# An mLSTM cell followed by a Fourier mix and an MLP: in batch 1, the order of the recurrence's products around the MLP's 64-feature products

## The chip, the cores and the metric

The kernel runs on one core of one Trainium2 chip. The metric is the device time of one execution in microseconds; the time before is the median of 11 runs. The profile is one further execution, in which the hardware profiler recorded every instruction.

The names used below are those of the profile: PE is TensorE (matmuls; PEld its weight loads), DVE is VectorE, ACT is ScalarE, POOL is GpSimd, SP is SyncE, whose queue issues all DMAs here. L465 is line 465 of the kernel before.

## What is computed

The reference has two parts. The first is a recurrence over 768 tokens for 4 batches of 8 heads with 40 features; the second, per batch, a Fourier transform over tokens and features, a normalization and an MLP with a residual.

```python
for t in range(S):                                  # mLSTM cell
    m_new = np.maximum(f_gate[:, :, t] + m, i_gate[:, :, t])
    f_stab, i_stab = np.exp(f_gate[:, :, t] + m - m_new), np.exp(i_gate[:, :, t] - m_new)
    C = f_stab * C + i_stab * np.einsum('bhd,bhe->bhde', vt, kt)
    n = f_stab * n + i_stab * kt
    h_tilde, nq = np.einsum('bhde,bhe->bhd', C, qt), np.einsum('bhd,bhd->bh', n, qt)
    y[:, :, t] = sigmoid(o_gate[:, :, t]) * h_tilde / np.maximum(np.abs(nq), 1.0)
...
u = x + np.real(np.fft.fft(np.fft.fft(x, axis=1), axis=2))   # x: y as (4, 768, 320)
un = (u - mean(u)) / np.sqrt(var(u) + 1e-06)
out = u + np.maximum(un @ w_ch1, 0.0) @ w_ch2                 # 320 -> 1280 -> 320
```

## The kernel before

**Chunks.** The recurrence isn't run token by token. A batch's 768 tokens are 6 chunks of 128, and each chunk needs, for its 8 heads: the *scores* of its keys with its queries (`mlstm_scores`, L465: 8 products with 40 rows, heads in pairs at partitions 0 and 64); a matrix of decays W (loaded by DMA, exponential on ACT in L421, cut to the causal half on POOL in L443 by `mlstm_mask`); the scores weighed by W (`mlstm_weigh`, DVE, L471); the queries times their decay, qg (`mlstm_scale_q`, POOL, L431); the *product with the state* (`mlstm_from_state`, L479: 4 full 128x128 products of C with qg); the *chunk outputs* (`mlstm_from_chunk`, L486: 8 products of the weighed scores with the values, 41 columns wide, into the same accumulator ph); and the *state update* (`mlstm_to_state`, L496: 8 products, 40 columns, into pc). The next state is made of the old one times its decay (`mlstm_decay`, POOL, L455) plus pc (`mlstm_gather`, DVE, L515; in chunk 0 a copy, L513). The same `mlstm_gather` copies ph to h on ACT (L517 to L529). `mlstm_turn` (L535) transposes h into px on PE, `mlstm_finish` (DVE, L544 to L550) divides and gates.

**The MLP's first layer.** In batch 0 it is done by `mlp_in`: 10 blocks of 128 hidden features for each of two groups of 3 chunks. The 320 inputs are 128 + 128 + 64, so a pair of blocks takes 4 full products (L837; 3 in the even slot, 1 in the odd one) and 2 products of 64 rows (L841, at partitions 0 and 64), called the 64-feature products. `mlp_relu` (ACT, L850) empties each pair.

**Order.** The kernel writes the order of all engines itself. `at(slot, phase, fn, ...)` puts a call into a table, and `run` goes through the table by slot and, in a slot, by phase; calls with the same key keep the order in which they were entered. The phases are EVAC = 0, FILL = 1, MAIN = 2, FILL_PE = 3, with fractions. Each engine executes its own instructions in the order so written. `plan_mlstm` enters a batch's recurrence; batch 1 begins at slot 32 with one chunk for every three slots, so that the scores of chunk c come in slot 32 + 3c, and the state product, the chunk outputs and the state update of chunk c three slots later, together with the next chunk's scores. Batch 0's `mlp_in` takes slots 31 to 50 in phase MAIN; the 64-feature products are in the even slots. Around them stand batch 0's last steps of the Fourier mix (L729 pu, L749 to L757 on DVE, L765 uc and L777 uT on ACT, the transpositions L772), the normalization factor (`mix_rstd`: L785 to L790 on DVE, then 12 small operations on POOL, L792 to L795, entered in slot 41), and the conversion of the second weight matrix from 64-bit floats (raw pieces by DMA; L344 and L346 on DVE, L351 and L352 on ACT, L358 to L364 on DVE).

**Buffers.** Two PSUM buffers (`ps_h`) are shared by ph, pc and px of all chunks, two (`ps_s`) hold scores, and four banks (`ps_m`) the rest; an instruction that writes a buffer waits for the last readers of what was in it.

Of the kernel before, what the change touches and what calls it, by code (L numbers as in the profile page):

```python
# [20 lines left out]
NT = S // L  # L21
# [29 lines left out]
def kernel(  # L51
# [70 lines left out]
    def at(slot, phase, fn, *args):  # L122
        plan.setdefault((slot, phase), []).append((fn, args))
# [7 lines left out]
    EVAC, FILL, MAIN, FILL_PE = range(4)  # L131
# [405 lines left out]
    def mlstm_finish(b, c):  # L537

        k = chunks.pop((b, c))
        if c == 0:  # L540
# [9 lines left out]
        nc.vector.tensor_tensor(out=xs[b][:, c, 0:DM].rearrange("p (h d) -> p h d", d=D), in0=h1[:, :, 0:D], in1=sc,  # L550
                                op=OP.mult)

    def plan_mlstm(b, s0, stride=3):
        for c in range(NT):
            s = s0 + stride * c
            if b > 0:
                t = 22 + 2 * c if b == 1 and c < 3 else s - 5
                at(t, FILL, mlstm_load, b, c)
                at(t, FILL, mlstm_load_max, b, c)
                at(t, FILL, mlstm_load_decay, b, c)  # L560
                at(s, FILL, mlstm_load_o, b, c)
            if (b, c) > (0, 0):
                at(s, FILL, mlstm_exp, b, c, 0)
                at(s + 1, FILL - 0.5, mlstm_exp, b, c, NP)
                last = (b, c) == (0, NT - 1)
                at(s - 1 if last else s, FILL_PE + (2.05 if last else 2), mlstm_scores, b, c)
                if b > 0:
                    at(s + 1, FILL, mlstm_mask, b, c)
            at(s, FILL, mlstm_scale_v, b, c)
            at(s if (b, c) == (0, 2) else s + 1, FILL + 0.1, mlstm_scale_q, b, c)  # L570
            at(s + 2, FILL, mlstm_decay, b, c)
            end = (b, c) == (0, NT - 1)
            at(s + 1 if end else s + 2, FILL - 0.4 if end else FILL, mlstm_weigh, b, c)
            at(s + 2 if end else s + 3, FILL_PE, mlstm_from_state, b, c)
            at(s + 2 if end else s + 3, FILL_PE + (2 if end else 3), mlstm_from_chunk, b, c)
            at(s + 3, FILL_PE + 3, mlstm_to_state, b, c)
            at(s + 3 if end else s + 4, FILL, mlstm_gather, b, c)
            if b == 0:
                t, x = ((8, 11), (11, 14), (13, 14), (14, 15.5), (17, 18), (18, 21))[c]
            else:  # L580
                t = s + (8, 8, 7, 5, 5, 5)[c]
                x = t + 1
            at(t, FILL_PE + ((2.5 if c < 4 else 1) if b == 0 else 1), mlstm_turn, b, c, b == 0 and c < 4)
            at(x, FILL + 0.05, mlstm_finish, b, c)


# [483 lines left out]
    def plan_batch(b, s_mlstm, s_mix, s_mlp):  # L1070
        plan_mlstm(b, s_mlstm)
        done = [s_mlstm + 3 * (j + NT // 2) + 7 for j in range(NT // 2)]
        assert s_mix >= done[-1] and s_mlp >= s_mix + 9
        late = [s_mlp + 2 * c for c in range(TG)]
        if b == 0:
            feat = [s_mix + 1, s_mix + 1, s_mlp + 3]
            turn = [s_mix + 2, s_mix + 3, s_mix + 4]
            add = turn + [s_mlp, s_mlp + 4, s_mlp + 6]
            late = [s_mlp + 2, s_mlp + 5, s_mlp + 7]
        else:  # L1080
            feat = [s_mix + c for c in ((3, 4, 6) if b == 1 else (3, 4, 7))]
            add = [s_mix + c for c in ((4, 4, 5, 6, 7, 7) if b == 1 else (4, 4, 5, 6, 8, 9))]
            turn = [s_mix + c for c in ((5, 6, 6) if b == 1 else (6, 7, 8))]
            late = [s_mix + c for c in ((7, 8, 8) if b == 1 else (9, 10, 10))]
            at(s_mlp, EVAC + 0.5, mlp_sums)
        plan_mix(b, s_mix, done, feat, add, turn + late)
        at(s_mlp + NFF, FILL + 0.6, mix_rstd, b)
        plan_mlp(b, s_mlp)
# [143 lines left out]
```

## Time and profile before

| What | us |
|---|---|
| Median of 11 runs | 421.61 |
| Lowest, highest | 421.40, 426.45 |
| Profiled execution, its own time | 421.59 |
| Span of the profiled execution | 419.9 |
| First to last full product of batch 0's first layer (L837) | 58.5 to 118.8 |

The span is the time between the first and the last recorded instruction; 1.69 us of the execution's time lie outside it.

In the stretch of the trace in which batch 0's first layer runs, the busy times were:

| Stretch, us | PE | PEld | DVE | ACT | POOL |
|---|---|---|---|---|---|
| 0 to 105 | 99.11 | 69.26 | 81.70 | 71.36 | 47.74 |
| 105 to 125 (20 us) | 19.36 | 12.62 | 18.99 | 11.18 | 8.38 |
| 125 to 150 (25 us) | 25.00 | 18.64 | 13.76 | 6.53 | 7.49 |

A timeline line gives start, duration, engine, line, operation, output and inputs, shape, and how many instructions were merged; what stands in brackets is the idle time of the engine before it and who ended it. Each fp32 matmul is recorded as two, so that "L837 x6" is three products. The durations of PE are modelled at their end; the distance from one start to the next is what was measured.

### The profile page before, as it was taken

How to read it: one execution, taken by the hardware profiler on the slowest of the kernel's cores; microseconds unless marked ns; L12 is line 12 of the kernel's file. 1: busy time of each engine (PE TensorE's matmuls, PEld its weight loads, DVE VectorE, ACT ScalarE, POOL GpSimd, SP SyncE). 2: the span in 40 equal slices, each digit the busy share in tenths (PEclk: the TensorE clock that was granted, in tenths of full speed). 3: DMA queues.
4: the chain of work that ended last, by engine and by line, in shares of the span. 5: the costliest groups of instructions: out<-in, count | busy, mean ns of one | idle time of the engine just before them, and what ended most of it. 6: DMA issues, size and time to landing. Idle time of an engine off the chain costs nothing.

```text
span 419.9 us, 8001 instructions
## 1 busy us (share of the span) xinstructions
PE 408.9 (97%) x2966; PEld 302.9 (72%) x2966; DVE 288.8 (69%) x682; ACT 189.5 (45%) x493; POOL 113.5 (27%) x194
## 2 busy tenths in 40 slices
PE   8999999999999999999999999999999999999997
PEld 6877555576667678776559998976559988455996
DVE  7789894767994738777765579788663786335652
ACT  6986276676562221664455413744441113355000
POOL 5654301459430620442131440341220000020000
PEclk9999999999999999999999999999999999999999
DMA  7789298557665254265100454210000000000010
GB/s 228 254 260 333 66 283 264 168 170 224 224 191 164 70 155 128 74 207 184 66 0 2 147 153 135 95 46 2 0 2 0 33 31 34 0 2 0 16 48 31
DMA packets 20549, 47.14 MB, mean 112 GB/s; under 512 B 2784, under 2 KB 9312, under 8 KB 20384
## 3 DMA queue, kind: packets, MB, share of 16 engines
q1 hardware_dynamic: 20512, 46.65, 35.6%
q8 instruction: 23, 0.38, 0.4%
q14 instruction: 14, 0.11, 0.1%
HBM read 42.52 MB, written 4.11 MB: 111 GB/s over the span
## 4 chain that ended last, share of the span: by engine, by line
PE 80%; DVE 9%; issue 3%; DMA 3%; ACT 2%; POOL 2%; ACTq 0%; DVEq 0%; POOLq 0%
PE pm L897 17%; PE po L999 17%; PE po L943 8%; PE pm L902 5%; PE ps L465 5%; PE ph L486 4%; PE ph L479 3%; PE pu L729 3%; PE pm L837 3%; PE px L535 2%; PE pz L698 2%; DMA kvt<-in_kv 1%; PE put L772 1%; PE pM L218 1%; PE pz L686 1%
## 5 line engine op out<-in xcount | busy, mean ns | idle before, releaser
L949 DVE SCALAR_TENSOR_TENSOR x<-po,rstd,x 128x160 f32<-128x160 f32 (+1 forms) x69 | 27.0, 394 | 40.5 <-PE po L999 34.1
L906 DVE TENSOR_TENSOR h<-h,pm 128x384 f32<-128x384 f32 x60 | 30.5, 550 | 30.5 <-ACT h L919 20.9
L421 ACT ACTIVATE W<-W,colT 128x128 f32<-128x128 f32 x144 | 45.0, 395 | 0.0
L443 POOL TENSOR_SCALAR_AFFINE_SELECT W<-W 128x1024 f32<-128x1024 f32 x18 | 21.5, 1197 | 79.8 <-ACT W L421 59.3
L943 PE MATMUL po<-w_sb,h 128*128 128x320 f32 x120 | 34.4, 435 | 0.0
L471 DVE TENSOR_TENSOR W<-ps,W 128x512 f32<-128x512 f32 x48 | 30.6, 679 | 4.2 <-POOL W L443 4.0
L897 PE MATMUL pm<-uT,w_sb 128*128 128x384 f32 x90 | 32.8, 492 | 0.2 <-DVE uT L885 0.2
L837 PE MATMUL pm<-uT,w_sb 128*128 128x384 f32 x80 | 29.8, 500 | 0.7 <-DVE x L749 0.5
L777 ACT COPY uT<-put 128x384 f32<-128x384 f32 x24 | 11.2, 478 | 40.2 <-PE put L772 40.2
L943 PEld LDWEIGHTS po<-w_sb,h 128*128 128x128 f32 x120 | 22.2, 190 | 9.5 <-issue 0.8
L999 PE MATMUL po<-T,S 128*128 128x160 f32 x180 | 27.9, 302 | 0.6 <-DVE x L949 0.6
L465 PE MATMUL ps<-qk 40*128 40x128 f32 x384 | 27.8, 284 | 0.0
L792 POOL TENSOR_TENSOR t<-rstd 128x6 f32<-128x6 f32 x12 | 3.0, 246 | 89.2 <-DVE v L790 88.6
L999 PEld LDWEIGHTS po<-T,S 128*128 128x128 f32 x180 | 25.5, 190 | 2.2 <-DVE x L949 1.0
L999 PE MATMUL po<-w_sb,h 128*128 128x160 f32 x180 | 26.4, 301 | 0.0
L465 PEld LDWEIGHTS ps<-qk 40*128 40x128 f32 x384 | 23.4, 187 | 4.2 <-issue 0.7
L999 PEld LDWEIGHTS po<-w_sb,h 128*128 128x128 f32 x180 | 25.1, 190 | 1.3 <-DVE x L949 0.3
L486 PE MATMUL ph<-W,kvt 128*41 128x128 f32 x384 | 25.8, 277 | 0.0
L524 ACT COPY h<-ph 41x512 f32<-41x512 f32 (+1 forms) x16 | 9.3, 583 | 35.7 <-PE ph L486 35.6
L431 POOL TENSOR_TENSOR qg<-qk,Gb 128x512 f32<-128x512 f32 x18 | 25.0, 1390 | 0.1
L479 PEld LDWEIGHTS ph<-qg,C 128*128 128x128 f32 x160 | 20.0, 191 | 6.3 <-issue 2.0
L897 PEld LDWEIGHTS pm<-uT,w_sb 128*128 128x128 f32 x90 | 16.2, 190 | 10.9 <-DVE h L906 1.5
(207 smaller groups left out, 866.8 us busy)
## 6 DMA issues: line engine op xcount, KB each, us to landing
W<-M_d SPq DMA_DIRECT2D x18, 512.0 KB
kvt<-in_kv SPq DMA_DIRECT2D x24, 324.0 KB
qk<-in_qkT SPq DMA_DIRECT2D x48, 160.0 KB
raw<-in_w SPq DMA_DIRECT2D x10, 640.0 KB
Gb<-G_d SPq DMA_DIRECT2D x36, 128.0 KB
so<-in_o SPq DMA_DIRECT2D x24, 160.0 KB
out<-x SPq DMA_DIRECT2D x24, 160.0 KB
ds_sb<-in_dft_s SPq DMA_DIRECT2D x1, 1155.0 KB
```

The costliest lines, as they stand in the source:

```text
L421: nc.scalar.activation(out=k.W[:, h, :], in_=M, func=AF.Exp, scale=-1.0, bias=colT[:, c, 0, b * H + h:b * H + h + 1])
L431: nc.gpsimd.tensor_tensor(out=k.qg, in0=k.qk[:, 0], in1=k.Gb, op=OP.mult)
L465: nc.tensor.matmul(k.ps[hip][:, p, :], k.qk[r, 1, p, :], k.qk[r, 0, p, :], start=True, stop=True)
L471: nc.vector.tensor_tensor(out=Wv, in0=k.ps[hip], in1=Wv, op=OP.mult)
L479: nc.tensor.matmul(k.ph[:, p, :], k.C[:, p, :], k.qg[:, p, :], start=(p == 0), stop=False, skip_group_check=True)
L486: nc.tensor.matmul(k.ph[hip * 64:hip * 64 + D1, p, :], k.v1[:, 2 * p + hip, :], k.W[:, 2 * p + hip, :], start=(c == 0 and p == 0), stop=Tr ...
L837: nc.tensor.matmul(k.pm[i], w1_sb[:, ch, f0:f0 + L], u[2 * ch], start=(ch == 0), stop=False)
L897: nc.tensor.matmul(bank, w, u, start=start, stop=True, skip_group_check=True)
L906: nc.vector.tensor_tensor(out=h, in0=h, in1=bank, op=OP.add)
L943: nc.tensor.matmul(k.po, hidden(gr, f)[:, i * L:(i + 1) * L], w2_sb[:, f, :], start=(f == 0), stop=(f == NFF - 1))
L949: nc.vector.scalar_tensor_tensor(out=u, in0=po, scalar=k.rstd[:, c:c + 1], in1=u, op0=OP.mult, op1=OP.add)
L999: nc.tensor.matmul(po, a[:, f], w[:, f], start=start and f == 0, stop=f == half - 1, skip_group_check=True)
```

## The change

In batch 1 alone (`b > 0`; the two lists of slots meet only batch 1's):

- `group(s)` moves slots 35 and 41 to 36 and 42. There the scores of chunks 1 and 3, and the chunk outputs and state updates of chunks 0 and 2 (with the gather behind them), run one slot later, behind the 64-feature products of that slot.
- In an even slot of batch 0's first layer, `mlstm_from_state` is entered at MAIN - 0.1, ahead of that slot's last full product, where it stood behind the 64-feature products (chunk 2's stood in slot 41, ahead of the scores of chunk 3, and is now in slot 42). This meets slots 36, 38, 42, 44 and 50 (in slot 36 chunk 0 has no product with the state). Slot 47 is odd and stays as it was.
- In a shifted slot's chunk the decay of the state on POOL is entered just behind the gather, and the gather at FILL + 0.05, behind the next chunk's weighing on DVE, behind the pair of `mlp_relu` or `mix` copies on ACT, and behind the next mask and qg on POOL.
- In an even slot `mlstm_turn` is entered at FILL_PE + 3.5 instead of FILL_PE + 1.

```diff
@@ -550,6 +550,14 @@
         nc.vector.tensor_tensor(out=xs[b][:, c, 0:DM].rearrange("p (h d) -> p h d", d=D), in0=h1[:, :, 0:D], in1=sc,
                                 op=OP.mult)
 
+
+
+    slots_of_halves = [s for s in range(32, 51, 2)]
+    shifted = (35, 41)
+
+    def group(s):
+        return s + (s in shifted)
+
     def plan_mlstm(b, s0, stride=3):
         for c in range(NT):
             s = s0 + stride * c
@@ -563,24 +571,26 @@
                 at(s, FILL, mlstm_exp, b, c, 0)
                 at(s + 1, FILL - 0.5, mlstm_exp, b, c, NP)
                 last = (b, c) == (0, NT - 1)
-                at(s - 1 if last else s, FILL_PE + (2.05 if last else 2), mlstm_scores, b, c)
+                at(s - 1 if last else group(s) if b > 0 else s, FILL_PE + (2.05 if last else 2), mlstm_scores, b, c)
                 if b > 0:
                     at(s + 1, FILL, mlstm_mask, b, c)
             at(s, FILL, mlstm_scale_v, b, c)
             at(s if (b, c) == (0, 2) else s + 1, FILL + 0.1, mlstm_scale_q, b, c)
-            at(s + 2, FILL, mlstm_decay, b, c)
+            at(s + 2, FILL + (0.1 if b > 0 and s in shifted else 0), mlstm_decay, b, c)
             end = (b, c) == (0, NT - 1)
+            g = group(s + 3) if b > 0 else s + 3
             at(s + 1 if end else s + 2, FILL - 0.4 if end else FILL, mlstm_weigh, b, c)
-            at(s + 2 if end else s + 3, FILL_PE, mlstm_from_state, b, c)
-            at(s + 2 if end else s + 3, FILL_PE + (2 if end else 3), mlstm_from_chunk, b, c)
-            at(s + 3, FILL_PE + 3, mlstm_to_state, b, c)
-            at(s + 3 if end else s + 4, FILL, mlstm_gather, b, c)
+            at(s + 2 if end else g, MAIN - 0.1 if b > 0 and g in slots_of_halves else FILL_PE, mlstm_from_state, b, c)
+            at(s + 2 if end else g, FILL_PE + (2 if end else 3), mlstm_from_chunk, b, c)
+            at(g, FILL_PE + 3, mlstm_to_state, b, c)
+            at(s + 3 if end else g + 1, FILL + (0.05 if g > s + 3 else 0), mlstm_gather, b, c)
             if b == 0:
                 t, x = ((8, 11), (11, 14), (13, 14), (14, 15.5), (17, 18), (18, 21))[c]
             else:
-                t = s + (8, 8, 7, 5, 5, 5)[c]
+                t = s + (8, 8, 7, 5, 5, 5)[c] + (c == NT - 1 and g > s + 3)
                 x = t + 1
-            at(t, FILL_PE + ((2.5 if c < 4 else 1) if b == 0 else 1), mlstm_turn, b, c, b == 0 and c < 4)
+            at(t, FILL_PE + ((2.5 if c < 4 else 1) if b == 0 else 3.5 if t in slots_of_halves else 1), mlstm_turn, b, c,
+               b == 0 and c < 4)
             at(x, FILL + 0.05, mlstm_finish, b, c)
 
 
```

## The prediction

> **What bounds the kernel now.** I read the page's busy times first, then the shares of the chain of waits, then the waits of PE, then the timelines of PE, DVE and POOL between 58 and 124 us, the stretch in which batch 0's first MLP layer and batch 1's recurrence run together. All of the change lies there: in the two built programs nothing before 69 us or after the last scores of this stretch changes its order.
>
> ```profile
> PE 408.9 (97%) x2966; PEld 302.9 (72%) x2966; DVE 288.8 (69%) x682; ACT 189.5 (45%) x493; POOL 113.5 (27%) x194
> PE 80%; DVE 9%; issue 3%; DMA 3%; ACT 2%; POOL 2%; ACTq 0%; DVEq 0%; POOLq 0%
> ```
>
> PE sets the time: what is taken off PE counts if PE doesn't wait instead. How a block's length depends on its neighbours is in PE's timeline:
>
> ```profile
> 61.27 0.92 PE L841 MATMUL pm<-uT,w1t_sb 64*128 64x384 f32 x4
> 62.02 1.06 PE L465 MATMUL ps<-qk 40*128 40x128 f32 x16
> 63.01 2.20 PE L837 MATMUL pm<-uT,w_sb 128*128 128x384 f32 x6
> ...
> 88.77 2.10 PE L837 MATMUL pm<-uT,w_sb 128*128 128x384 f32 x6
> 90.70 1.05 PE L479 MATMUL ph<-qg,C 128*128 128x128 f32 x8
> 91.69 1.16 PE L465 MATMUL ps<-qk 40*128 40x128 f32 x16
> 92.78 1.07 PE L486 MATMUL ph<-W,kvt 128*41 128x128 f32 x16
> 93.68 0.47 PE L496 MATMUL pc<-vw,kvt 128*40 128x41 f32 x16
> 94.09 0.91 PE L837 MATMUL pm<-uT,w_sb 128*128 128x384 f32 x2
> 94.93 0.92 PE L841 MATMUL pm<-uT,w1t_sb 64*128 64x384 f32 x4
> 95.78 2.20 PE L837 MATMUL pm<-uT,w_sb 128*128 128x384 f32 x6
> 97.82 0.60 PE L535 MATMUL px<-ident,h 128*128 128x128 f32 x4
> 98.25 0.81 PE L837 MATMUL pm<-uT,w_sb 128*128 128x384 f32 x2
> 98.99 0.92 PE L841 MATMUL pm<-uT,w1t_sb 64*128 64x384 f32 x4
> 100.08 1.16 PE L479 MATMUL ph<-qg,C 128*128 128x128 f32 x8 [0.17 <-POOL qg L431]
> ```
>
> Read the distances from start to start. The 64-row products (L841) take 0.75 us before scores (61.27 to 62.02), but 0.85 before a full product (94.93 to 95.78). Scores (L465) take 0.99 behind 64-row products (62.02 to 63.01), but 1.09 behind full ones (91.69 to 92.78). A single full product (L837 x2) takes 0.84 behind L496, 0.74 behind L535. So each change between full, 64-row and 41-column products costs about 0.1 us on leaving and 0.1 on entering, 0.2 together.
>
> The last line is the one to remember: the product with the state of chunk 3 (L479) already waits 0.17 us for POOL's qg. What it will wait for in the new order:
>
> ```profile
> 97.55 0.19 POOL L521 COPY h<-h_first 128x4 f32<-128x4 f32 x1
> 97.69 1.09 POOL L443 TENSOR_SCALAR_AFFINE_SELECT W<-W 128x1024 f32<-128x1024 f32 x1
> 98.75 1.27 POOL L431 TENSOR_TENSOR qg<-qk,Gb 128x512 f32<-128x512 f32 x1
> ```
>
> ```profile
> 94.41 0.67 DVE L515 TENSOR_TENSOR C<-C,pc 40x164 f32<-40x164 f32 x2
> 98.82 1.29 DVE L471 TENSOR_TENSOR W<-ps,W 128x512 f32<-128x512 f32 x2 [1.59 <-POOL W L443]
> ```
>
> POOL masks W (L443) and only then multiplies qg (L431); DVE updates the state of chunk 2 (L515) at 94.41, long before it weighs chunk 3 (L471), which waits for that mask.
>
> [...] The weight load of scores at 61.70 lies 0.32 us ahead of its first matmul behind 64-row products, against none at 91.69: that is the 0.1 on entering. [...] POOL's small rstd operations of 128x6 (L792 to L795), 0.20 us at the median, take up to 0.81 from 92.18 to 94.60, while DVE does its two-input SBUF operations. [...]
>
> **The change part by part.** Chunks 0 and 2 of batch 1 now run scores, chunk outputs and state update one slot later (36 and 42), behind the 64-row products; in slots 38, 44 and 50 the order already was that, but the state product (L479) stood in between and now goes before the last full product. In all five places "full, scores, 41-column, full, 64-row, full" (or "full, 64-row, full, 64-row, 41-column, full") becomes "full, 64-row with scores, 41-column, full": five changes of mode become three. Two fewer, 2 x 0.2 = 0.4 us each, **2.0 us in all**. No product, weight load or DMA is added or removed; SP's order is the same. The turn of slot 40 moves in name only (nothing else stands there).
>
> Now the waits, walked along each engine's own order with the durations of before; old time in brackets.
>
> *Chunk 0, slot 36.* PE: last full product 71.67, 64-row 72.41, scores 73.16, L486 74.15, L496 75.05, transposition put 75.46 [76.21]. ACT no longer copies h (1.17 us) and so (0.47) ahead of uc, so uc is done at about 74.1, and put doesn't wait (0.28 before). DVE's copy L513 (0.69) moves behind the weighing, so L344, L346, L743, L744, L749 end at about 76.2 [77.14]; the next full product waited 0.53 for L749 and starts at 76.33 [77.28]. Gain here 0.95. The raw DMA for L344 was issued at 62.46, and no DMA runs between 72.5 and 74, so it has landed.
>
> *Chunk 1, slot 38.* L479 now needs the state copy L513, which stands behind L749's statistics and the weighing of chunk 1: 76.85 + 1.27 + 0.69 gives 78.75. PE is there at 76.33 + 1.97 = 78.3: a new wait of 0.45. Then L479 0.99, full product 0.74, 64-row 0.75, scores 0.99, L486 0.90, L496 0.41: put at 83.55 [84.37]. Gain 0.82. L526 on POOL now waits for the later h (78.5), but mask and qg stand ahead of it now; nothing urgent is behind.
>
> *Chunk 2, slots 41 and 42.* px at 87.45, full products 87.95, L479 at 89.88. Its qg: POOL's L431 of chunk 2 hangs on put (uT, relu, exp, mask), so it too comes 0.82 earlier, 88.95: no wait. Full product 90.77, 64-row 91.5, scores 92.25, L486 93.25, L496 94.15, full products of slot 43 at **94.56 [95.78]**. Gain 1.22.
>
> *Chunk 3, slot 44.* This is where I expect it to be given back. PE finishes those three products and px at 94.56 + 2.04 + 0.43 = 97.03, and L479 is next; before, a full product and the 64-row products (0.74 + 0.85) stood in between. L479 now waits for two things. POOL: rstd's 12 operations began at 92.18 and ended at 97.61; their start hangs on DVE's L790 behind the weighing of chunk 2 and so on put: 0.82 earlier, ending at about 96.8. L521 (0.14 in the queue) is now behind. The mask L443 runs to about 97.95, qg to 99.2. DVE is worse: L515 of chunk 2 now stands *behind* the weighing of chunk 3 (and behind the take L344 of a raw piece), which needs that mask: 97.95 + 0.03 + 1.25 + 0.67 gives **99.9 [100.08]**. L479 waits about 2.85 us.
> From there: L479 0.99, full 0.74, 64-row 0.75: scores of chunk 4 at 102.38 [101.16], L486 103.37, L496 104.27, slot 45 at 104.68 [103.56]. Loss 1.12. On ACT the second half of exp of chunk 4 is behind relus that wait for the later 64-row products (end 102.4), so the mask of chunk 4 ends near 105.9 [103.55]; DVE reaches that weighing only at about 106.6 [107.87], so it costs nothing.
>
> *Slots 46 to 50.* Before, L479 of chunk 4 waited 0.64 us for L550 at 110.72. Now PE is there at 111.17, and L550 is done by about 109.7: the old wait covers part of the loss, and PE is 0.31 late there, 0.24 at the scores. Slot 50's two modes save 0.4 (its qg at about 114.9 and L515 at about 116 are both before 118.7). At 123 us PE is **0.16 us ahead**.
>
> Sum: 5 x 0.4 = 2.0 saved, old waits of 0.28 + 0.53 + 0.17 + 0.64 = 1.6 gone, new waits of 0.45 and 2.85 with an exposed weight load at 0.1 each: -3.6 + 3.5 = **-0.1 to -0.2 us**. After 123 us PE waits in one more place over 0.3 us (0.43 at 266); I carry the difference to the end. The profiled execution took 421.59 us for a span of 419.9; the median is 421.61. The span becomes 419.7, the time **421.4**.
>
> Bounds of what before doesn't show. The saving in each of the five places: 0.2 to 0.4 (one pair of 64-row products and scores is seen, at 61.27; I take 0.4). L479 between full products: 0.89 to 1.09; I take 0.99 after a wait. The rstd chain: from 3.4 us (12 at 0.28 apart, as its undisturbed middle runs) to 7; I take 5.4, since L358 to L364 stand beside its start as before. That alone moves the wait at chunk 3 by -2.0 to +1.6.
>
> **Rivals.**
> 1. *The gain stays* (18%). The wait at chunk 3 is over a microsecond shorter, because rstd runs undisturbed. For: 7 of 12 operations already take 0.20 to 0.23. Against: the same DVE operations follow L790. With L479 at 98.0 the whole is -2.0: **419.6**.
> 2. *The wait at chunk 3 is longer* (16%). Place: POOL's queue between L790 and L443, and L344 ahead of L515 on DVE. Price: one for one. It decides from L479 at 101.3, when rstd ends 1.4 us later than walked, or the raw piece (issued 90.98, landed 95.86; now gated by qg of chunk 2 and about 0.9 earlier) lands after 99. At 101.9: **423.4**. Against: with nothing moved forward at all, L479 starts at 100.75, and the whole is +0.7, still no change.
> 3. *PE's clock falls in that wait* (10%). [...] The longest wait after the start is 0.82 us here, and PEclk is 9 throughout, so no run shows it[...]: **423.1**.
> The likeliest, gain given back at chunk 3, has 56%; its own range is 420.6 to 422.5.
>
> **Numbers.** What a measurement tells from no change is 0.3%, 1.26 us. Faster 0.19 (rival 1 and a tail), same 0.55, slower 0.26 (rivals 2 and 3). Range for 8 in 10: 420.0 to 423.4.
>
> **What would show it.** Scores at 0.99 and 64-row products at 0.75 in five places; L837 of slot 37 near 76.3; L479 of chunk 1 waiting under 1 us for DVE; L479 of chunk 3 waiting 2 to 3.5 us for L515; no wait of L479 at chunk 4; PE at L943 near 123.2 [123.33]. I am wrong if L479 of chunk 3 waits under 1.5 us, if another wait over 0.5 us appears, or if PEclk drops.

## The result and the profile after

The changed kernel takes 424.49 us (median of 13 runs, 422.40 to 426.28), the kernel before, timed beside it, 422.14 (50 runs): a ratio of 1.0054 with a 95% interval of 1.0039 to 1.0069. It is slower by 2.3 us; forecast was no change. The profiled execution took 426.02 us for a span of 424.3, 4.4 us more than before's 419.9. In what follows the lines behind L583 have moved by ten: L837 of before is L847 after, L749 is L759, L792 to L795 are L802 to L805.

The page of the changed kernel: busy times, the row of the granted TensorE clock (tenths, 40 slices of 10.6 us) and the shares of the chain of waits.

```profile
PE 409.9 (97%) x2966; PEld 305.1 (72%) x2966; DVE 288.7 (68%) x682; ACT 189.4 (45%) x493; POOL 113.7 (27%) x194
PEclk9999999898999999999999999999999999999999
PE 81%; DVE 7%; DMA 4%; issue 3%; ACT 3%; POOL 2%; ACTq 0%; POOLq 0%; DVEq 0%
```

PE is busy for one microsecond *more* than before (408.9), with the same 2966 matmuls and, in each of five places, two changes of mode fewer. The row of the granted clock (its share of full speed) is what a reader should look at first here: two slices show an 8, so some of the busy time was spent at a lower clock.

The waits of PE, longest first (total us, times, longest):

```profile
PE ph L479 <- DVE C L515: 2.8, 1, 2.8
PE pm L847 <- DVE x L759: 2.1, 1, 2.1
```

The first was forecast, the second was not. Both are in PE's timeline:

```profile
72.67 0.92 PE L851 MATMUL pm<-uT,w1t_sb 64*128 64x384 f32 x4
73.42 1.06 PE L465 MATMUL ps<-qk 40*128 40x128 f32 x16
74.41 1.07 PE L486 MATMUL ph<-W,kvt 128*41 128x128 f32 x16
75.32 0.47 PE L496 MATMUL pc<-vw,kvt 128*40 128x41 f32 x16
75.72 0.55 PE L782 MATMUL put<-ident,uc 128*128 128x128 f32 x3
78.34 3.78 PE L847 MATMUL pm<-uT,w_sb 128*128 128x384 f32 x6 [2.08 <-DVE x L759]
81.92 1.18 PE L479 MATMUL ph<-qg,C 128*128 128x128 f32 x8
...
97.75 2.20 PE L847 MATMUL pm<-uT,w_sb 128*128 128x384 f32 x6
99.79 0.60 PE L535 MATMUL px<-ident,h 128*128 128x128 f32 x4
103.14 2.05 PE L479 MATMUL ph<-qg,C 128*128 128x128 f32 x8 [2.76 <-DVE C L515]
```

Three things stand here. The saving is real: 64-row products to scores 0.75 us, scores to chunk outputs 0.99 (72.67, 73.42, 74.41), and the same in the other four places. The first layer of slot 37 starts at 78.34, where 76.33 was forecast. And what follows each wait is slow: the three full products of 78.34 take 3.58 us to the next start, those of 97.75 take 2.04; L479 at 103.14 takes 2.05 for eight records, at 81.92 it takes 1.18.

How slow, the table by stretch shows (start and end, length, PE, PEld, DVE, ACT and POOL busy with their instructions, granted clock, DMA share, GB/s), the 3.4 us ahead of and behind the two places where the clock falls:

```profile
75.34:78.75 3.41, 1.33 (x25) 0.94 (x20) 3.29 (x6) 2.41 (x6) 1.48 (x2) 1.00 0.49 175
78.75:82.17 3.42, 3.42 (x8) 1.91 (x7) 3.35 (x7) 3.37 (x8) 1.68 (x4) 0.50 0.77 253
99.24:102.65 3.41, 1.15 (x7) 0.60 (x5) 2.25 (x5) 2.62 (x6) 3.13 (x5) 1.00 0.71 218
102.65:106.06 3.41, 2.92 (x10) 2.21 (x10) 3.23 (x8) 0.00 (x0) 1.88 (x3) 0.50 0.58 130
```

In the stretch ahead PE is busy for 1.33 and 1.15 us of 3.41, in the stretch behind the clock is half. The second fall comes at 102.65, while PE still waits; L479 starts at 103.14.

**Who was late in slot 37.** DVE's timeline (L344 and L346 take a raw piece of the second weight matrix apart):

```profile
74.34 1.26 DVE L344 TENSOR_SCALAR e<-raw 128x640 uint32<-128x640 uint32 x1
75.53 1.55 DVE L346 TENSOR_SCALAR m<-raw 128x640 uint32<-128x640 uint32 x1
77.01 0.31 DVE L753 COPY pu<-pu 1x160 f32<-1x160 f32 x1
77.35 0.32 DVE L754 COPY pu<-pu 1x161 f32<-1x161 f32 x1
77.71 0.49 DVE L759 TENSOR_TENSOR x<-x,pu 128x320 f32<-128x320 f32 x1
```

Before, L344 and L346 took 0.49 us each, at 75.01 and 75.42. The reason is on POOL:

```profile
73.91 1.35 POOL L443 TENSOR_SCALAR_AFFINE_SELECT W<-W 128x1024 f32<-128x1024 f32 x1 [7.79 <-ACT W L421]
75.23 1.50 POOL L431 TENSOR_TENSOR qg<-qk,Gb 128x512 f32<-128x512 f32 x1
78.66 0.19 POOL L526 COPY h_first<-h 128x4 f32<-128x4 f32 x1 [1.93 <-ACT h L524]
```

The gather of chunk 0, with its small copy L526, used to stand ahead of the mask of chunk 1 on POOL and waited for ACT's copy until 75.22; mask and qg then began at 75.51 and 76.83. The change puts the copy behind them, so that they run as soon as the exponentials are there, at 73.91 and 75.23: 1.6 us earlier, right beside L344 and L346. Each of these two ends 0.34 or 0.35 us after the POOL instruction beside it (75.60 against 75.26, 77.08 against 76.73).

The profile before had this already, at another place, where L344 ran beside qg:

```profile
30.68 1.52 POOL L431 TENSOR_TENSOR qg<-qk,Gb 128x512 f32<-128x512 f32 x1
31.51 1.04 DVE L344 TENSOR_SCALAR e<-raw 128x640 uint32<-128x640 uint32 x1
```

It ended at 32.55, 0.35 us behind qg. In slot 36 of before, L346 started at 75.42, 0.09 us ahead of the mask (75.51), and kept its 0.49.

**Who was late at chunk 3.** The normalization factor's 12 operations on POOL (the first at 94.55) end where the mask of chunk 3 begins; the weighing L471 on DVE waits for the mask, and L515 stands behind the weighing:

```profile
94.55 0.78 POOL L802 TENSOR_TENSOR t<-rstd 128x6 f32<-128x6 f32 x1 [0.52 <-DVE v L800]
...
100.00 1.09 POOL L443 TENSOR_SCALAR_AFFINE_SELECT W<-W 128x1024 f32<-128x1024 f32 x1
101.12 1.29 DVE L471 TENSOR_TENSOR W<-ps,W 128x512 f32<-128x512 f32 x2 [1.14 <-POOL W L443]
102.33 0.67 DVE L515 TENSOR_TENSOR C<-C,pc 40x164 f32<-40x164 f32 x2
```

### The profile page after: what moved, and what is told of

It reads as the page before. It is cut to its first block, busy times and chain, and to the rows that moved or that the text cites. A ratio compares the mean times of both kernels' runs of the same rounds, so it can differ in the third digit from the quotient of the medians.

```text
span 424.3 us, 7999 instructions
## 1 busy us (share of the span) xinstructions
PE 409.9 (97%) x2966; PEld 305.1 (72%) x2966; DVE 288.7 (68%) x682; ACT 189.4 (45%) x493; POOL 113.7 (27%) x194
## 4 chain that ended last, share of the span: by engine, by line
PE 81%; DVE 7%; DMA 4%; issue 3%; ACT 3%; POOL 2%; ACTq 0%; POOLq 0%; DVEq 0%
PE po L1009 18%; PE pm L907 17%; PE po L953 8%; PE pm L912 5%; PE ps L465 5%; PE ph L486 4%; PE ph L479 4%; PE pu L739 3%; PE pm L847 3%; PE px L535 2%; DMA raw<-in_w 2%; PE put L782 2%; PE pz L708 2%; DMA kvt<-in_kv 2%; PE pz L696 1%
## 5 line engine op out<-in xcount | busy, mean ns | idle before, releaser
L953 PE MATMUL po<-w_sb,h 128*128 128x320 f32 x120 | 34.4, 435 | 0.0
L847 PE MATMUL pm<-uT,w_sb 128*128 128x384 f32 x80 | 31.8, 527 | 2.4 <-DVE x L759 2.1
L471 DVE TENSOR_TENSOR W<-ps,W 128x512 f32<-128x512 f32 x48 | 30.7, 680 | 4.9 <-POOL W L443 4.7
L907 PE MATMUL pm<-uT,w_sb 128*128 128x384 f32 x90 | 32.8, 492 | 0.2 <-DVE uT L895 0.2
L953 PEld LDWEIGHTS po<-w_sb,h 128*128 128x128 f32 x120 | 22.2, 190 | 9.5 <-issue 0.8
L802 POOL TENSOR_TENSOR t<-rstd 128x6 f32<-128x6 f32 x12 | 2.9, 246 | 89.2 <-DVE v L800 88.6
L479 PEld LDWEIGHTS ph<-qg,C 128*128 128x128 f32 x160 | 21.2, 200 | 7.0 <-POOL h L521 3.0
L479 PE MATMUL ph<-qg,C 128*128 128x128 f32 x160 | 22.5, 285 | 3.6 <-DVE C L515 2.8
L431 POOL TENSOR_TENSOR qg<-qk,Gb 128x512 f32<-128x512 f32 x18 | 24.9, 1384 | 0.1
```

Source lines behind the costliest of these rows:

```text
L431: nc.gpsimd.tensor_tensor(out=k.qg, in0=k.qk[:, 0], in1=k.Gb, op=OP.mult)
L471: nc.vector.tensor_tensor(out=Wv, in0=k.ps[hip], in1=Wv, op=OP.mult)
L479: nc.tensor.matmul(k.ph[:, p, :], k.C[:, p, :], k.qg[:, p, :], start=(p == 0), stop=False, skip_group_check=True)
L847: nc.tensor.matmul(k.pm[i], w1_sb[:, ch, f0:f0 + L], u[2 * ch], start=(ch == 0), stop=False)
L907: nc.tensor.matmul(bank, w, u, start=start, stop=True, skip_group_check=True)
L953: nc.tensor.matmul(k.po, hidden(gr, f)[:, i * L:(i + 1) * L], w2_sb[:, f, :], start=(f == 0), stop=(f == NFF - 1))
```

## Experiments

All edits are to the changed kernel unless it is said otherwise; times of the kernel before in the same jobs are 421.87 (e1 to e4), 421.75 (e5 to e8) and 422.00 us (e9 to e11).

### e2: move the raw piece's conversion away from POOL's mask

```diff
-    when += [((s, 0.7), (s + 1, 0.7), (s + 2, 0.6)) for s in (33, 36, 39, 42, 45)]
+    when += [((37, 0.06) if s == 36 else (s, 0.7), (s + 1, 0.7), (s + 2, 0.6)) for s in (33, 36, 39, 42, 45)]
```

> The changed kernel, with one step of the weight conversion (L344 and L346 of the raw piece of slot 36) moved on DVE behind the residual addition L759, the weighing of chunk 1 and the state copy L513. Theory (the first wait comes from L344 and L346 meeting POOL's mask and qg of chunk 1, 2.8 us instead of 0.9): L759 ends near 75.8, the wait of L847 in slot 37 falls from 2.08 to under 0.4 us, no clock drop there; the second wait stays at 2 to 3 us with its clock drop in part of the runs: 421.2 to 423. Rival (the residual addition is late for another reason, such as the DVE queue ahead of it): the wait stays over 1.5 us and the time within 0.7 us of the changed kernel.

Measured: 421.76 us (419.44 to 423.23, 22 runs), ratio 0.9988 (0.9974 to 1.0002). DVE in slots 36 and 37:

```profile
74.10 0.31 DVE L753 COPY pu<-pu 1x160 f32<-1x160 f32 x1
...
74.80 0.49 DVE L759 TENSOR_TENSOR x<-x,pu 128x320 f32<-128x320 f32 x1
75.32 0.50 DVE L766 BATCH_NORM_STATS2 stats<-x 128x6 f32<-128x320 f32 x1
...
77.84 0.49 DVE L344 TENSOR_SCALAR e<-raw 128x640 uint32<-128x640 uint32 x1
78.25 0.48 DVE L346 TENSOR_SCALAR m<-raw 128x640 uint32<-128x640 uint32 x1
```

POOL's mask (73.78, 1.35 us) and qg (75.10, 1.27 us) run at the same time as in the changed kernel. L753, L754 and L759, which have an input from PSUM, keep their durations beside them, and so does L766, which reads SBUF (0.50 beside qg, 0.49 in the changed kernel); L344 and L346, moved to where POOL has nothing, are back at 0.49 and 0.48. PE's first layer of slot 37 starts at 75.97 with no wait. The edit takes all of their 2.81 us out of the way, of which 1.83 are the lengthening; their 0.98 at the old lengths could not have made a wait of 2.08. That POOL is what lengthens them is seen in the times above and again in e6 to e8. So the meeting of L344 and L346 with POOL is the cause of the new wait.

That the median now is what was forecast for the change is partly luck: the other wait (2.71 us for L515) is still there, and in this profile the clock still falls behind it, which the forecast had only among its rivals; and the wait of 0.45 for L513 that the forecast had is gone in e2.

### e1: fill both waits with work for PE

The transpositions ahead of each wait are done several times over, with the same result: those of slot 36 five times, those of chunk 1's turn six times.

```diff
-        for ch in range(3):
+        for ch in [*range(3)] * (5 if (b, c) == (0, 2) else 1):
...
-        for p in range(NP):
+        for p in [*range(NP)] * (6 if (b, c) == (1, 1) else 1):
```

> The changed kernel, with the two long waits of PE filled by repeating transpositions that stand just ahead of them (the put of slot 36 five times instead of once, the px of chunk 1 six times), into the same PSUM tile and with the same result. No engine is asked to do anything earlier. Theory A (the loss is mostly the clock, which is halved for about 3.4 us after each of the two waits, 1.7 us each): no slice of PEclk under 1.0, L847 of slot 37 and L479 of chunk 3 at full speed (three full products in 2.0 us, L479 x8 in 1.0), and 2 to 3 us less than the changed kernel's 424.5: 421.5 to 422.5, with runs that lie within 1.5 us of each other. Rival B (the loss is the waits themselves): PE is no further at the end of either wait than without the filling, so the time stays at 424 to 425.

Measured: 423.47 us (422.39 to 424.73, 21 runs), ratio 1.0031 (1.0020 to 1.0042), between what theory and rival had given. The clock was 1.00 throughout, and in all 21 executions the mean granted clock was 0.999 or more. PE's timeline:

```profile
75.49 1.86 PE L782 MATMUL put<-ident,uc 128*128 128x128 f32 x15
78.11 2.17 PE L847 MATMUL pm<-uT,w_sb 128*128 128x384 f32 x6 [0.77 <-DVE x L759]
...
98.45 2.78 PE L535 MATMUL px<-ident,h 128*128 128x128 f32 x24
101.80 1.13 PE L479 MATMUL ph<-qg,C 128*128 128x128 f32 x8 [0.56 <-DVE C L515]
```

PE starts the first layer of slot 37 as late as in the changed kernel (78.11), but at full speed. From there to the start of slot 43's products (97.75 in the changed kernel, 96.41 here) PE gains 1.1 us, from L479 of chunk 3 to the start of slot 45's (109.31 and 106.55) 1.4. The profiled execution is 2.6 us shorter (423.43 against 426.02): that is what two stretches of half clock cost where both come.

Not every execution has both. The mean granted clock of an execution is on record: 0.999 or 1.000 where the trace shows no stretch at half clock (e3, e10), 0.996 with one (e2, e11), 0.991 with the two of the changed kernel's profile; single executions have 0.995 and 0.992 as well, which I count as one and two. By this measure 2 of its 14 executions had two stretches (425.95 and 426.02 us), 9 had one (median 424.53) and 3 had none (422.40, 422.42 and 423.52). So the typical one has a single stretch. By the medians of e1 and the changed kernel the clock is worth 1.0 of the 2.3 us; by the groups of executions one stretch goes with 2.1, and what is left is close to the kernel before (422.14). Three executions are few, and longer waits may be what brings the falls, so that the groups may differ in their waits too: the clock's share of the typical 2.3 us lies between these two and isn't settled.

### e3: the normalization factor later, e10: the other conversion later

The wait of L479 of chunk 3 has two candidates ahead of L515: POOL's chain of 12 small operations in front of the mask, and the raw piece's L344 on DVE. e3 enters the factor's chain four slots later; e10 moves the conversions of slots 36 and 42 and leaves the chain.

```diff
# e3
-        at(s_mlp + NFF, FILL + 0.6, mix_rstd, b)
+        at(s_mlp + NFF + (4 if b == 0 else 0), FILL + 0.6, mix_rstd, b)
# e10
-    when += [((s, 0.7), (s + 1, 0.7), (s + 2, 0.6)) for s in (33, 36, 39, 42, 45)]
+    when += [((s + 1, 0.06) if s in (36, 42) else (s, 0.7), (s + 1, 0.7), (s + 2, 0.6)) for s in (33, 36, 39, 42, 45)]
```

> The changed kernel, with batch 0's normalization factor (L795 to L800 on DVE and 12 small operations on POOL) entered in slot 45 instead of 41, behind the mask and qg of chunks 3 and 4. Theory (the wait of L479 at chunk 3 hangs on POOL's queue of rstd, mask, then DVE's weighing and L515): the wait falls from 2.76 to about 1.5 us, where DVE's L344, which waits for a raw piece by DMA, takes over as its cause; the first wait is as before the edit: 422 to 423.3. Rival (L344 behind its DMA sets it already, POOL is not the cause): the wait stays over 2.4 us and the time within 0.7 us of the changed kernel.

Measured: 422.12 us (419.64 to 424.36, 22 runs), ratio 1.0003 (0.9987 to 1.0019). The wait of chunk 3 falls from 2.76 to 1.07 us; that of slot 37 stays at 2.07 us, and in this profile the clock did not fall behind it.

> The changed kernel with both takes (slots 36 and 42) one slot later, the normalization factor where it was. Theory (the wait of L479 of chunk 3 is set by POOL: the factor's chain, mask L443, then weighing and L515 on DVE; the take's L344 ended at 99.58, before the mask did): the wait stays at 2.3 to 2.8 us, no wait for L759 in slot 37, and the time is that of e2, 421.2 to 421.8. Rival (L344 ahead of the weighing is what makes DVE late, or it slows the mask): the wait falls under 1.5 us and the time to about 420.3.

Measured: 421.05 us (419.30 to 422.32, 22 runs), ratio 0.9976 (0.9965 to 0.9988). PE's timeline shows what is left:

```profile
99.03 1.13 PE L479 MATMUL ph<-qg,C 128*128 128x128 f32 x8 [2.26 <-DVE C L515]
```

The time is just below the stretch that the theory gave, but the wait of 2.26 us is there: with L344 out of the way the chain on POOL alone still makes it. The chain is the main cause (1.7 us of the wait, by e3; the 1.07 left there stands behind L344, which waits for its raw piece). L344 is worth the 0.45 between 2.71 (e2) and 2.26, and that goes through POOL: beside L344 and L346 two of the factor's small operations take 0.51 and 0.33 us in e2, against 0.19 and 0.20 in e10, and the chain from its start to the mask takes 5.40 and 4.95.

### e4, e5 and e9: the same edits on three orders

e4 has the edits of e3 and e10 together. e5 has the same edits on the kernel before. e9 has them on the changed kernel without the shift of chunks 0 and 2, so that only slots 38, 44 and 50 are changed.

```diff
# e9 in addition
-    shifted = (35, 41)
+    shifted = ()
```

> The edits of the two runs before together, and the step L344 and L346 of slot 42 moved behind L515 as well. Theory: both waits fall under 0.8 us, no slice of PEclk under 1.0, the mode changes saved (2.0 us) and the old waits gone stay: 419 to 420.5, faster than the kernel before. Rival (the new order of products costs on PE itself, or moves its wait elsewhere): 421.5 or more with no wait over 1 us in the two places.

> The kernel BEFORE, with the three edits of the fastest run so far (the factor rstd in slot 45, the takes of slots 36 and 42 one slot later behind the DVE work of the recurrence), but without the change. Theory (the change's order of products is worth its 2 us of mode changes once its waits are gone): 420.5 to 422, that is 2.5 to 4 us above the 417.8 of the same edits with the change. Rival (the three edits are worth it alone, and the change adds nothing): 417.5 to 419.

> The changed kernel with the three edits of e4, but without the shift of chunks 0 and 2 (shifted is empty): the change acts in slots 38, 44 and 50 alone. Theory (each place is worth two mode changes of 0.2 us, 0.4 in all, wherever PE has no wait to fall into): 3 x 0.4 = 1.2 us under e5's 419.81, so 418.6, and 0.8 above e4's 417.83. Rival (the saving comes mostly from the two shifted chunks): about 419.4. Rival (the shift is worth nothing once the waits are gone): 417.8.

| Order, with the three edits | us, median (runs) | ratio, interval | against e5 |
|---|---|---|---|
| before (e5) | 419.81 (6) | 0.9939 (0.9916 to 0.9961) | |
| changed, no shift (e9) | 418.64 (5) | 0.9929 (0.9915 to 0.9944) | -1.17 |
| changed (e4) | 417.83 (5) | 0.9887 (0.9862 to 0.9911) | -1.98 |

I missed e5: the edits help the kernel before by 1.9 us, more than expected, since it too had waits near these instructions; those of 0.53, 0.17 and 0.64 us are gone in e5's trace, that of 0.28 is still there. e4 came out 1.2 us below the least that I had expected. The three kernels ran in three different jobs, five or six executions each, and the intervals of the ratios of e5 and e9 overlap, so the last column alone proves little. The traces show it directly. From the start of slot 43's full products to slot 45's PE takes 7.56 us in e5 (95.58 to 103.14) and 7.16 in e9 (94.70 to 101.86) and e4 (94.22 to 101.38); from the transpositions put of slot 36 to those of slot 38 7.40 in e5 and 7.01 in e9; from slot 49's full products to the first L943 (L953) 7.25 in e5 and 6.86 in e9; around the shifted chunk 2 7.01 in e5 (88.57 to 95.58) and 6.62 in e4 (87.60 to 94.22). The fifth place, chunk 0's, has waits in both. So a place is worth 0.4 us where PE doesn't wait, which is the two changes of mode at 0.2 us that the prediction counted. PE in e4 around chunk 3:

```profile
96.26 0.60 PE L535 MATMUL px<-ident,h 128*128 128x128 f32 x4
96.69 1.06 PE L479 MATMUL ph<-qg,C 128*128 128x128 f32 x8
```

L479 follows the transpositions with no wait, and the clock is 1.00 in the profile. e4 beats both kernels, the one before by 1.1% (ratio 0.9887).

### e6, e7 and e8: parts of the change

`shifted` is set to () in e6, (41,) in e7 and (35,) in e8.

> The change with no chunk moved to another slot (scores, chunk outputs and state updates of slots 35 and 41 stay); only the product with the state goes ahead of the last full product in slots 38, 44 and 50. Theory: three places save 0.4 us each, the first wait doesn't arise (POOL's mask of chunk 1 stays behind L526), L515 of chunk 2 keeps its place ahead of the weighing of chunk 3, so L479 of chunk 3 waits for POOL's qg, 1.5 to 2 us, mostly without a clock drop: 421 to 422.2, about the kernel before. Rival (the state product ahead of the last full product is what costs): 423.5 or more.

> The change with slot 41 moved to 42 but slot 35 left in its place. Theory: no wait over 0.6 us in slot 37 and no clock drop there, since POOL's mask of chunk 1 stays behind L526 and L344, L346 take 0.9 us again; L479 of chunk 3 waits 2.4 to 3 us for L515 behind the weighing, with a clock drop in part of the runs: 421.8 to 423.3. Rival (the loss is in chunk 3's part): 424 or more.

> The change with slot 35 moved to 36 but slot 41 left in its place. Theory: the wait of L847 in slot 37 is there with about 2 us for L759 behind L344 and L346 of together 2.8 us, with a clock drop in part of the runs; L479 of chunk 3 waits 1 to 2 us for qg (L515 ahead of the weighing): 422.5 to 424.2. Rival (the loss is in chunk 3's part): 421.5 or less.

| Shifted | us, median (runs) | ratio, interval | L847, slot 37, waits | L479, chunk 3, waits |
|---|---|---|---|---|
| none (e6) | 421.90 (22) | 0.9995 (0.9984 to 1.0007) | 0.52 for L759 | 1.60 for qg (L431) |
| chunk 2 (e7) | 422.83 (22) | 1.0020 (1.0007 to 1.0033) | 0.52 for L759 | 3.95 for L515 |
| chunk 0 (e8) | 422.57 (14) | 1.0015 (0.9997 to 1.0034) | 2.08 for L759 | 1.47 for qg (L431) |

Each wait belongs to one shift: chunk 0's brings the one in slot 37 (L344 and L346 take 1.26 and 1.55 us in e8, 0.49 each in e6 and e7), chunk 2's turns the wait for qg at chunk 3 into a longer one for L515. With no shift at all, the 1.2 us of three places are still used up by the wait for qg, which the changed order of L479 alone makes longer (0.17 before). The profiled executions of e6 and e7 are the slowest of their 22. In e7 the wait of chunk 3 is longer than the 2.4 to 3 us that I had expected, 3.95, for in it the raw piece landed just as POOL began the mask (96.18, 1.09 us) and qg (97.23, 1.50 us), and L344 and L346 met them once more, so that the weighing of chunk 3 began at 99.01 and not at the mask's end, 97.27:

```profile
96.46 1.15 DVE L344 TENSOR_SCALAR e<-raw 128x640 uint32<-128x640 uint32 x1 [2.92 <-DMA raw<-in_w]
97.53 1.55 DVE L346 TENSOR_SCALAR m<-raw 128x640 uint32<-128x640 uint32 x1
```

In e7's profile the clock was half from 99.78 to 106.61, for twice 3.41 us.

### e11: one more step on e4

e4's trace still has a wait of 1.10 us of PE for ACT's relu at 71 us, behind ACT's share of the conversion (it differs from trace to trace: 0.20 in the changed kernel, 0.81 in e5, none in e9). e11 moves that share, and the joining on DVE (L358 to L364), one slot later for the piece of slot 33.

```diff
# inside the line of e10, cut
-... (s + 1, 0.7), (s + 2, 0.6) ...
+... (s + 1 + (s == 33), 0.7), (s + 2 + (s == 33), 0.6) ...
```

> e4 with the conversion and join of slot 33's raw piece one slot later on ACT and DVE, so that ACT's relu L860 at 71 us isn't behind them. Theory (PE is bound and that wait is the last one over 0.6 us near there): the wait of 1.10 us ahead of slot 35's product falls under 0.3 us and the time by about 0.8 us to 417.0. Rival (the conversion collides with the next piece's on ACT and DVE one slot later, and the wait comes back there): 417.8 or more.

Measured: 419.86 us (419.05 to 421.09, 6 runs), ratio 0.9956 (0.9939 to 0.9973), 2.0 us *above* e4. The rival had the right mechanism, with another partner. The relu's wait is gone, but the joining now stands beside POOL's mask and qg. DVE:

```profile
72.30 1.71 DVE L360 SCALAR_TENSOR_TENSOR m<-raw,m 128x640 f32<-128x640 uint32 x1
74.05 1.78 DVE L364 TENSOR_TENSOR w_sb<-m,e 128x640 f32<-128x640 f32 x1
```

and POOL:

```profile
71.66 1.67 POOL L443 TENSOR_SCALAR_AFFINE_SELECT W<-W 128x1024 f32<-128x1024 f32 x1 [6.16 <-ACT W L421]
73.31 1.84 POOL L431 TENSOR_TENSOR qg<-qk,Gb 128x512 f32<-128x512 f32 x1
```

All four are long (L360 and L364 take 0.82 us in e4), PE waits 1.90 us for L759 again, and the clock falls behind that wait. It is the failure of the changed kernel made a second time, by another pair of instructions. This too stood in the profile before: beside mask and qg of chunk 4, L360 (102.52) and L364 (104.26) took 1.71 and 1.78 us.

## Why the prediction was wrong

**The step that failed** is chunk 0, slot 36: "DVE's copy L513 (0.69) moves behind the weighing, so L344, L346, L743, L744, L749 end at about 76.2 [77.14]". The order was right, the durations were not. I carried L344 and L346 over at the 0.49 us that they had before. In the part on chunk 1 I even wrote that mask and qg now stand ahead of L526 on POOL, but only asked who is behind them, not when they would run now: 1.6 us earlier, beside L344 and L346. L759 ended at 78.20 and not 76.2, and the first layer of slot 37 started 2.0 us late. e2 shows it, by taking only this meeting away: L344 and L346 are back at 0.49 and 0.48 us. That POOL's small operations are longer beside DVE's (0.20 us at the median, up to 0.81) had been used, and the other direction had been left out. The durations of L344 in the profile before, up to 1.04 us, could have told it.

**The second miss** is rival 3's price and its 10%: PEclk is 9 throughout in the profile before, so both were my estimates, with no measured fall behind them. In the changed kernel the clock was halved behind waits of 2.08 and 2.76 us, with PE busy for 39% and 34% of the 3.41 us ahead; the last section has the other traces. Two falls came, of 1.1 and 1.4 us.

**The sum, done again for the profiled execution**: -0.15 forecast, +2.0 for slot 37, +2.5 for the clock (1.1 and 1.4) make +4.35; measured 4.4. Without the clock: -0.15 + 2.0 = +1.85; e1 measured 423.47 - 421.87 = +1.6, the three executions of the changed kernel without a fall lie at +0.3, +0.3 and +1.4. Without the wait of slot 37 the forecast was 421.4. e2 measured 421.76, a median over 13 executions with a fall of the clock (median 422.21) and 9 without (420.35), and its trace is without the forecast's wait of 0.45: two errors of the forecast nearly cancel there.

**What was right.** Two changes of mode fewer at five places, 2.0 us in all: 0.4 in each of the four places that the traces of e4, e5 and e9 show without waits. L479 of chunk 3 would wait 2.85 us for L515, behind the weighing, the mask and the factor's chain: 2.76, and e3 and e10 show the chain as its main cause. The wait of 0.64 at chunk 4 would go: it did. Of the chain on POOL I took 5.4 us, measured 94.55 to 100.00, 5.45. The wait of 0.45 at chunk 1 isn't seen in the changed kernel, where PE was slow at that time, but is 0.35 in e1, e3 and e8. The raw piece of rival 2 did land late (L344 at 99.05, waiting 2.19 us for it), but ahead of the mask's end at 101.09; it was not waited for, and cost about the 0.45 of e10, by slowing the factor's chain. "PE 0.16 us ahead at 123" was 4.4 behind.

**The range** (420.0 to 423.4) lies below the result, since I had asked of each stall what is late next, but held all durations fixed except in the rstd chain; the rivals' sum had no case in which a *saved* wait moves POOL's work onto DVE's.

## What to carry to other kernels

When an instruction of POOL moves forward in its queue, look up what DVE does at its new time before carrying any duration over, and look at the longest duration of the same instruction in the profile before, not only at the usual one: `tensor_scalar` from SBUF to SBUF went from 0.49 to 1.3 and 1.6 us here, operations that read PSUM did not change (L759 took 0.49 us beside the mask in e2). A reorder that shortens PE's work pays only if the producers keep up, so mend their order first (the three edits of e4) and the same reorder is worth its full 2.0 us. Price a long wait of PE with the clock in mind: here the shortest with a fall behind it was 1.90 us (e11), and a fall cost 1.1 and 1.4 us more than the wait itself.

## What the runs showed of the hardware

- **Half clock behind waits of 1.90 to 3.95 us, but not behind every one.** Behind waits of 1.90 (e11), 2.08 (changed kernel), 2.71 (e2), 2.76 (changed kernel) and 3.95 us (e7) the clock was half; behind waits of 2.07 and 2.08 us in e3 and e8 it was not, nor behind 2.26 in e10. The recorded changes of the clock lie whole multiples of 3.413 us apart: in the changed kernel, whose record of the clock begins at 7.07 us, it is full for 71.68 us (21 of them), half for one, full for 20.48 (6), half for one, full for 317.44 (93); in the profile before it is full for 413.01 (121), in e7 half for two (99.78 to 106.61). In this grid it fell behind windows in which PE was busy for 0.70 to 1.52 us of 3.41. Two pairs of windows, one ahead of an edge and one behind it, in e11 (the fullest that was followed by a fall) and in e3 (the emptiest that was not):

```profile
73.67:77.08 3.41, 1.52 (x33) 1.25 (x30) 3.27 (x6) 1.85 (x5) 1.48 (x1) 1.00 0.42 136
77.08:80.49 3.41, 3.40 (x6) 1.90 (x7) 3.31 (x8) 1.37 (x3) 1.34 (x4) 0.50 0.91 220
74.32:77.73 3.41, 1.80 (x37) 1.51 (x35) 3.34 (x5) 1.57 (x4) 2.26 (x2) 1.00 0.42 130
77.73:81.14 3.41, 2.60 (x10) 1.51 (x11) 3.28 (x8) 3.37 (x9) 0.97 (x3) 1.00 0.78 218
```

Of the windows that began at full clock, those with 0.70 (e2 and e7), 1.15 and 1.33 (changed kernel) and 1.52 us (e11) of PE were followed by a fall; behind 1.80 (e3), 2.08 and 2.17 (e8), and behind all with 2.59 us or more in the profiles of before and of the changed kernel, the clock stayed full. What lies between 1.52 and 1.80 us was not measured. From half clock it rose after 2.92 and 3.42 us (changed kernel), and stayed at half after 2.18 (e7). Two waits of the same length differ in how the edges cut them: in the changed kernel the 2.08 us of slot 37 (76.27 to 78.34) lie in one window, and the clock fell; in e3 the edge at 77.73 cuts the 2.07 us (76.12 to 78.19), and it did not. By the mean granted clock, falls came in 11 of 14 executions of the changed kernel, 13 of 22 of e2, 13 of 22 of e7, 9 of 22 of e10, 7 of 22 of e3, 2 of 6 of e11, 1 of 14 of e8, 1 of 22 of e6 (longest wait there 1.60 us), 2 of 137 of the kernel before in the same jobs and in none of the 37 of e1, e4, e5 and e9. Why e8 has so few isn't shown.

- **DVE's `tensor_scalar` with SBUF on both sides took longer beside POOL's mask and qg.** 128x640 (L344, L346): 0.49 us alone, 1.26 and 1.55 beside the two in the changed kernel and in e8. Not every DVE operation that reads SBUF did: the batch-norm statistics L766 kept 0.50 beside qg in e2. Two-input ones (L360, L364 in e11): 0.82 alone, 1.71 and 1.78, and POOL's two were slower as well (1.67 and 1.84 us, against 1.35 and 1.27 in e2).
- **A change of mode (between full, 64-row and 41-column fp32 products) was worth 0.2 us here**, 0.1 on leaving (the 64-row products of before take 0.85 us ahead of a full product, 0.75 ahead of scores) and 0.1 on entering (scores 1.09 behind full products, 0.99 behind 64-row ones): 0.39 or 0.40 us for two of them in each of the three places of e9 against e5, 1.98 for ten by the medians of e4 and e5, which ran in different jobs.
